# Three engines in hardware loops, DMA buffers moved to a 512-byte boundary, and a finer last load, in a decode kernel that streams a KV cache

## Chip, cores, metric

The kernel runs on one core of a Trainium2 chip. The metric is the device time of one execution in microseconds (us). A ratio is the mean time of one kernel's runs over the mean time of the other's runs in the same rounds, so it is not quite the ratio of the medians that are quoted beside it.

## The reference

One decode step, batch 2, one query position: an attention branch over a cache of 32768 keys and values (8 KV heads, 32 query heads), and a small MLP branch that gates its result.

```python
def _A_ref(x, k_cache, v_cache, wq, wo):        # caches: (2, 8, 32768, 128) bf16
    q = ((x @ wq).reshape(B, Sq, Hq, Dh)).transpose(0, 2, 1, 3)
    k = jnp.repeat(k_cache, rep, axis=1); v = jnp.repeat(v_cache, rep, axis=1)
    p = _softmax(jnp.einsum("bhqd,bhkd->bhqk", q, k) * (Dh ** -0.5))
    o = jnp.einsum("bhqk,bhkd->bhqd", p, v)
    return o.transpose(0, 2, 1, 3).reshape(B, Sq, Hq * Dh) @ wo
xn = _layernorm(A_x)
return A_x + _A_ref(xn, ...) * _silu(_B_ref(xn, ...))   # _B_ref: the MLP branch
```

K and V are 16 groups (batch x KV head) of 8.4 MB each. With the weights, 280.5 MB have to be read once.

## The kernel before

SyncE issues all large loads, in the order wq, w3, w4, K0, V0, K1, V1, ... K15, V15, wo. For one group, VectorE transposes K in 16 pieces, TensorE makes the scores, ScalarE the exponentials, VectorE transposes them, TensorE multiplies by V, and a short chain of copies, small matmuls and VectorE operations turns the sum into a column of `oX`. After the last group `oX` is multiplied by wo. TensorE runs 15 groups in a hardware loop and the last one unrolled; VectorE and ScalarE are unrolled over all 16.

```python
WO_PARTS = [(0, 4, 0, 2048), (4, 7, 0, 2048), (7, 8, 0, 2048)]
...
kbuf = pers.tile([128, 3 * SLOT], BF16, name="kbuf")     # first tile of the pool
vbuf = pers.tile([128, 2 * SLOT], BF16, name="vbuf")
...                                                       # SyncE
wait(sp, k_h2)
load_v(0)
for m in range(1, NG):
    wait(sp, (p_t, NT * (m - 1) + NR))                    # K's shared slot is free
    load_k(m)
    wait(sp, (p_o, m))                                    # V of the group before is used up
    load_v(m)
wait(sp, (p_t, NT * last))
for i, (g0, g1, c0, c1) in enumerate(WO_PARTS):
    d_wo[i].after(sp.dma_start(out=wo3[:, g0:g1, c0:c1], in_=wos[:, g0:g1, c0:c1]), 16)
...                                                       # VectorE, unrolled
for m in range(NG):
    for i in range(NPART):
        ...
        for r in range(NR):
            n = NT * m + NR * i + r
            wait(dve, (p_t, n + 1 - T_BUFS))
            dve.transpose(out=Ts[n % T_BUFS]..., in_=kt...).then_inc(s_t, 1)
    ...
...                                                       # TensorE
with pe.Fori(0, last):
    scores()
    values(lambda h: take(pe, s_v, 16) if h == 0 else None)
scores()
values(lambda h: wait(pe, (d_vl[h], 16)))
wait(pe, k_oX)
for i, (g0, g1, c0, c1) in enumerate(WO_PARTS):
    wait(pe, (d_wo[i], 16))
    ...                                                   # 16 matmuls a group of wo
```

`take(eng, sem, n)` waits until a semaphore is at least n and takes n off it, so that the same code can run for every group.

The softmax here doesn't subtract the row's maximum and nothing guards it: scores larger than these inputs give would overflow.

## Time and profile before

| | before |
|---|---|
| median of 4 runs | 661.09 us (660.90 to 661.62) |
| span of the profiled run | 659.8 us |
| load queue, share of 16 DMA engines' span | 98.5% |
| instruction packets inside the span (q8 + q14) | 5 + 6 |
| last V half used from | 645.00 us |
| `oX` complete | 652.44 us |

The page of the profile. First the busy time of each engine, then the row of 40 slices for the DMA engines (9 is 90% busy or more), then the DMA queues: q1 carries the loads, q8 and q14 carry instructions.

```profile
PE 393.7 (60%) x2684; PEld 165.5 (25%) x2684; DVE 337.0 (51%) x428; ACT 50.3 (8%) x152; POOL 5.7 (1%) x18
...
DMA  8999999999999999999999999999999999999994
...
q1 hardware_dynamic: 6408, 280.50, 98.5%
q8 instruction: 5, 0.08, 0.1%
q14 instruction: 6, 0.05, 0.0%
```

No compute engine is near its limit, the DMA engines are. Between 3 and 650 us their mean busy share is 1.00, as the windows show (DMA share and GB/s are the last two columns):

```profile
3.00:650.00 647.00, 388.65 (x2547) 160.90 (x2548) 334.69 (x418) 50.13 (x152) 3.95 (x8) 0.81 1.00 432
```

The end of the kernel, from the timeline (start in us, duration, engine, line, operation; in brackets the idle time before it and what ended it). L503 is the product with V, L473 completes `oX`, L540 is the product with wo:

```profile
645.00 3.59 PE L503 MATMUL bank<-vbuf,pt 128*16 128x512 bf16 x32 [5.08 <-DMA vbuf<-in_A_v_cache_dram]
...
652.27 0.17 DVE L473 TENSOR_REDUCE oX<-xm 128x4 bf16<-128x16 f32 x1
...
652.50 3.58 PE L540 MATMUL bank<-kbuf,oX 128*2 128x128 bf16 x128 [0.47 <-DVE oX L473]
```

TensorE waits 5 us for the last half of V, and everything after is a chain. The chain that ended last says the same, and that wo is not waited for:

```profile
652.27 0.18 DVE oX L473
652.45 0.04 issue
652.50 3.61 PE bank L540 x96
```

Two things are not on the page but in the trace's records of completion counts and of DMA packets. First the counts. The trace has 16 counts for each load of K, V and weights, as many as there are chains of load packets (below), and a load is used when the last of them has come: the last V half has its first count at 640.80 us and its 16th at 644.96, and TensorE starts on it at 645.00. I take one count for one DMA engine. So for each load there is a time when the 9th engine is done and one when the 16th is. Their difference, here called the lag, is how far the slowest engine is behind the middle:

```
kernel before, in us        load 1 (K0)   10th   11th   20th   21st   29th   30th   34th (last V half)
lag, 16th minus 9th count       1.5        1.5    1.9    1.9    2.9    2.9    3.9     4.0
VectorE instruction packets:  48 us            232 us        424 us        604 us
```

The loads are 19.35 us apart, and the lag grows only in the load in which a VectorE instruction packet arrives. (The queues are put down to engines by the doses below: unrolling VectorE takes q14 from 2 packets to 7, unrolling TensorE q8 from 4 to 22.)

Second, the packets. Their records name no engine, but from 22.5 to 640 us each packet begins within 0.05 us of the end of another, so the sixteen chains of packets, one for each DMA engine, can be followed. This is a stretch of the chain with the VectorE packet at 232 us (packets of 4 bytes left out):

```
start, us   took, ns   queue   bytes      one DMA engine of the kernel before
  230.093       2422   q1      65536
  232.512        333   q14      8192      instructions of VectorE
  232.833       3080   q1      65536      0.66 us longer than the others
  235.916       2419   q1      65536
```

The packet's own time and the lengthening of the load packet behind it together cost this engine 0.98 us. The VectorE packets at 48, 232, 424 and 604 us all lie in this one chain; the one at 188 us lies in another, and costs that engine 0.68 us.

### The profile page before, as it was taken

How to read it: one execution, taken by the hardware profiler on the slowest of the kernel's cores; microseconds unless marked ns; L12 is line 12 of the kernel's file. 1: busy time of each engine (PE TensorE's matmuls, PEld its weight loads, DVE VectorE, ACT ScalarE, POOL GpSimd, SP SyncE). 2: the span in 40 equal slices, each digit the busy share in tenths (PEclk: the TensorE clock that was granted, in tenths of full speed). 3: DMA queues.
4: the chain of work that ended last, by engine and by line, in shares of the span. 5: the costliest groups of instructions: out<-in, count | busy, mean ns of one | idle time of the engine just before them, and what ended most of it. 6: DMA issues, size and time to landing. Idle time of an engine off the chain costs nothing. (4 is left out here: it accounts for less than half of the span.)

```text
span 659.8 us, 6521 instructions
## 1 busy us (share of the span) xinstructions
PE 393.7 (60%) x2684; PEld 165.5 (25%) x2684; DVE 337.0 (51%) x428; ACT 50.3 (8%) x152; POOL 5.7 (1%) x18
## 2 busy tenths in 40 slices
PE   0538195683829558282865828376481947648765
PEld 0513132231313223031322303132131322213223
DVE  2347191744809165380926539083562908447650
ACT  0111001010100101010010101001010010101000
POOL 1200000000000000000000000000000000000000
PEclk9999787785978769597885959779596976959795
DMA  8999999999999999999999999999999999999994
GB/s 366 434 443 441 434 445 421 421 445 433 441 442 405 441 434 441 441 445 401 441 433 445 441 413 429 438 441 441 441 401 445 433 445 437 417 429 430 421 421 197
DMA packets 6443, 280.64 MB, mean 425 GB/s; under 512 B 664, under 2 KB 672, under 8 KB 1696
## 3 DMA queue, kind: packets, MB, share of 16 engines
q1 hardware_dynamic: 6408, 280.50, 98.5%
q8 instruction: 5, 0.08, 0.1%
q14 instruction: 6, 0.05, 0.0%
q10 hardware_dynamic: 24, 0.01, 0.0%
HBM read 280.50 MB, written 0.00 MB: 425 GB/s over the span
## 5 line engine op out<-in xcount | busy, mean ns | idle before, releaser
L486 PE MATMUL bank<-T,z 128*128 128x512 bf16 x1024 | 283.1, 428 | 184.7 <-PEq L45 179.6
L449 DVE STREAM_TRANSPOSE T<-kbuf 128x1024 int32<-128x1024 int32 x256 | 290.6, 1206 | 150.5 <-DMA kbuf<-in_A_k_cache_dram 150.5
L486 PEld LDWEIGHTS bank<-T,z 128*128 128x128 bf16 x1024 | 99.3, 104 | 362.0 <-issue 283.6
L503 PE MATMUL bank<-vbuf,pt 128*16 128x512 bf16 x1024 | 68.2, 426 | 5.1 <-DMA vbuf<-in_A_v_cache_dram 5.1
L466 DVE RECIPROCAL rec<-bank 128x4 f32<-128x4 f32 x16 | 2.9, 182 | 114.2 <-PE bank L513 114.2
L423 ACT ACTIVATE ep<-bank 128x512 bf16<-128x512 f32 x32 | 19.1, 598 | 482.2 <-PE bank L486 482.2
L503 PEld LDWEIGHTS bank<-vbuf,pt 128*16 128x16 bf16 x1024 | 26.4, 98 | 38.8 <-issue 12.6
L457 DVE STREAM_TRANSPOSE pt<-ep 128x512 bf16<-128x512 bf16 x32 | 22.1, 691 | 20.2 <-ACT ep L423 20.2
L496 PE MATMUL bank<-sm,ones_f 128*128 128x4 f32 x64 | 9.4, 252 | 27.6 <-PEq L45 27.6
L513 PE MATMUL bank<-sel_o,ob 128*128 128x4 f32 x128 | 17.2, 258 | 12.5 <-PEq L45 12.5
L513 PEld LDWEIGHTS bank<-sel_o,ob 128*128 128x128 f32 x128 | 16.3, 199 | 20.5 <-issue 20.5
L496 PEld LDWEIGHTS bank<-sm,ones_f 128*128 128x128 f32 x64 | 8.5, 192 | 35.4 <-issue 35.4
L431 ACT COPY ob<-bank 128x512 f32<-128x512 f32 x16 | 9.4, 586 | 87.6 <-PE bank L503 87.6
L411 ACT COPY z<-qr 32x16 bf16<-32x16 bf16 x64 | 12.6, 197 | 0.6
L286 PE MATMUL bank<-ident,xn_bf 2*128 2x2 bf16 x4 | 0.3, 166 | 16.7 <-POOL x L277 16.7
L519 PE MATMUL bank<-on,sel_r 128*128 128x4 bf16 x64 | 3.9, 164 | 9.0 <-PEq L45 9.0
L423 ACT ACTIVATION_READ_ACCUMULATOR ep<-bank 128x1 f32 x32 | 6.3, 198 | 0.2
L470 DVE TENSOR_TENSOR xm<-bank,mask 128x16 f32<-128x16 f32 x16 | 2.8, 175 | 6.8 <-PE bank L519 6.8
L245 DVE CAST xf<-x_bf 128x512 f32<-128x512 bf16 x1 | 0.4, 427 | 11.4 <-DMA x_bf<-in_A_x_dram 11.4
L462 DVE TENSOR_SCALAR sm<-sel_h,rs 128x4 f32<-128x4 f32 x32 | 6.0, 188 | 0.0
L519 PEld LDWEIGHTS bank<-on,sel_r 128*128 128x128 bf16 x64 | 2.9, 97 | 9.9 <-issue 9.9
L322 PE MATMUL bank<-xT,kbuf 128*128 128x2 bf16 x128 | 3.6, 165 | 2.0 <-DVE xT L316 2.0
(64 smaller groups left out, 50.2 us busy)
## 6 DMA issues: line engine op xcount, KB each, us to landing
kbuf<-in_A_k_cache_dram SPq DMA_DIRECT2D x2, 4096.0 KB, 23.7
vbuf<-in_A_v_cache_dram SPq DMA_DIRECT2D x2, 4096.0 KB, 28.9
kbuf<-in_A_wq_dram SPq DMA_DIRECT2D x1, 4096.0 KB, 12.2
vbuf<-in_B_w_dram SPq DMA_DIRECT2D x2, 1792.0 KB, 17.9
kbuf<-in_A_wo_dram SPq DMA_DIRECT2D x1, 2048.0 KB, 38.3
kbuf<-in_A_wo_dram SPq DMA_DIRECT2D x1, 1536.0 KB, 41.5
kbuf<-in_A_wo_dram SPq DMA_DIRECT2D x1, 512.0 KB, 42.1
kbuf<-in_A_k_cache_dram SPq DMA_DIRECT2D x15, 27.7
```

The lines of the kernel that those rows point to most:

```text
L322: i = pe.matmul(qT_ps[:, h * B:(h + 1) * B], lhsT=wq3[:, k, h * Dh:(h + 1) * Dh], rhs=xT[:, k, :], start=(k == 0), stop=(k == DK - 1),)
L411: i = act.copy(out=z[32 * j:32 * j + 32, :, :, c:c + rep], in_=qr[32 * j:32 * j + 32, :, :, b, g * rep:(g + 1) * rep],)
L423: act.activation(out=eps_[i][:, :], in_=sc[i][:, :], func=ACT.Exp, scale=inv_sqrt_dh, accum_out=rss[NPART * (m % 2) + i][:, :],)
L431: act.copy(out=ob[:, :], in_=o[:, :]).then_inc(s_ob, 1)
L449: dve.transpose(out=Ts[n % T_BUFS][:, :].rearrange("p (b t k) -> p t b k", b=NB, t=RT), in_=kt[:, r * W:(r + 1) * W].rearrange("p (t b k) ...
L457: dve.transpose(out=pts[h][:, :, :].rearrange("p r (t h) -> p t r h", h=rep), in_=eps_[i][:, :].rearrange("p (t r h) -> p t r h", r=NR, h= ...
L462: dve.tensor_scalar_mul(out=sms[h][:, :], in0=sel_h[:, :], scalar1=rss[NPART * (m % 2) + i][:, 0:1]).then_inc(s_p, 1)
L486: last_mm = pe.matmul(sc[i][:, :], lhsT=z[:, nb, e, zc:zc + 128], rhs=Tb[:, nb, :, e], start=(r == 0 and nb == 0 and e == 0), stop=(r == N ...
L496: pe.matmul(S, lhsT=ones_f[:, :], rhs=sms[h][:, :], start=(h == 0), stop=(h == NPART - 1))
L503: last_mm = pe.matmul(o[32 * j:32 * j + VT * rep, :], lhsT=pts[h][:, r, a * VT * rep:(a + 1) * VT * rep], rhs=vt[:, u * VT:(u + 1) * VT, : ...
L513: last_mm = pe.matmul(oT, lhsT=ob[:, t * Dh:(t + 1) * Dh], rhs=sel_o[:, t, :], start=(t == 0), stop=(t == VT - 1))
L519: last_mm = pe.matmul(xp[:, r, :], lhsT=sel_r[:, r, :, :].rearrange("p j w -> p (j w)"), rhs=on[:, :], start=True, stop=True,)
```

## The change

Its intent: run TensorE, VectorE and ScalarE over all 16 groups in hardware loops (VectorE two groups a turn, because K's halves alternate), so that their code is not streamed during the run; put the DMA buffers on a 512-byte boundary; cut wo's last pieces finer, so that less work follows the last landing. All waits inside the loops become semaphores that are taken down, and since each matmul of this program signals one semaphore, one-column matmuls (`mark`) signal the others.

```diff
-WO_PARTS = [(0, 4, 0, 2048), (4, 7, 0, 2048), (7, 8, 0, 2048)]
+WO_PARTS = [(0, 2, 0, 2048), (2, 4, 0, 2048), (4, 5, 0, 2048), (5, 6, 0, 2048), (6, 7, 0, 2048),
+            (7, 8, 0, 1024), (7, 8, 1024, 1536), (7, 8, 1536, 2048)]
+    pers.tile([128, PAD // 4], F32, name="pad")          # PAD = 384
     kbuf = pers.tile([128, 3 * SLOT], BF16, name="kbuf")
 ...
-            wait(sp, (p_t, NT * (m - 1) + NR))
+            sp.wait_ge(p_k, m)
             load_k(m)
-            wait(sp, (p_o, m))
+            sp.wait_ge(p_o, m)
             load_v(m)
 ...
-        emit_z(0)
-        for m in range(NG):
+        with act.Fori(0, NG) as m:
+            for j in range(4):  ...  in_=qr[..., bass.ds(m * rep, rep)]
 ...
-        for m in range(NG):
-            ...  wait(dve, (p_t, n + 1 - T_BUFS))
+        with dve.Fori(0, NG // 2) as t:
+            for odd in range(2):
+                group(odd, t)          # inside: take(dve, s_tf), take(dve, s_k[i], 16), ...
 ...
-        with pe.Fori(0, last):
-            scores(); values(...)
-        scores(); values(...)
+        with pe.Fori(0, NG):
+            ...  mm.then_inc(s_tf if r < NR - 1 else s_sc, 1)
+            ...  mark(s_tf); if i == 0: mark(p_k)
```

In the built programs kbuf starts at byte 16512 of a partition before (128 past a multiple of 512) and at 16896 (a multiple) after.

More of the change, by code (lines that the diff above doesn't have):

```diff
@@ L18 @@
 T_BUFS = 4
+PAD = 384
 GELU_C = 0.7978845608028654
 EPS = 1e-5
-WO_PARTS = [(0, 4, 0, 2048), (4, 7, 0, 2048), (7, 8, 0, 2048)]
+WO_PARTS = [(0, 2, 0, 2048), (2, 4, 0, 2048), (4, 5, 0, 2048), (5, 6, 0, 2048), (6, 7, 0, 2048), (7, 8, 0, 1024), (7, 8, 1024, 1536), (7, 8, 1536, 2048)]
 class Count:
@@ L100 @@
     pts = [pers.tile([128, NR, RT * rep], BF16, name=f"pt{i}") for i in range(NPART)]
-    rss = [pers.tile([128, 1], F32, name=f"rs{i}") for i in range(2 * NPART)]
+    rss = [pers.tile([128, 1], F32, name=f"rs{i}") for i in range(NPART)]
     sms = [pers.tile([128, rep], F32, name=f"sm{i}") for i in range(NPART)]
@@ L107 @@
     xm = pers.tile([128, NQ, rep], F32, name="xm")
-    oX = pers.tile([128, Hkv, NQ, B], BF16, name="oX")
+    oX = pers.tile([128, B * Hkv * NQ], BF16, name="oX")
     ident = pers.tile([128, 128], BF16, name="ident")
@@ L125 @@
     q_sb = pers.tile([128, B, Hq], BF16, name="q_sb")
-    qr = pers.tile([128, NB, 2, B, Hq], BF16, name="qr")
+    qr = pers.tile([128, NB, 2, B * Hq], BF16, name="qr")
     hf = pers.tile([128, FK * B], F32, name="hf")
@@ L149 @@
     qr_ps = sc[1][:, 0:NB * 2 * B * Hq].rearrange("p (n e c) -> p n e c", n=NB, e=2)
+    mark_ps = treg_b[0:1, 0:1]
     hT = xp_b[:, 0:FK * B]
@@ L158 @@
         d_x, d_wq, d_w3, d_w4 = (Count(nc, n) for n in ("d_x", "d_wq", "d_w3", "d_w4"))
-        d_k = [Count(nc, f"d_k{i}") for i in range(2)]
-        d_kl = [Count(nc, f"d_kl{i}") for i in range(NPART)]
-        s_v = nc.alloc_semaphore("s_v")
-        d_vl = [Count(nc, f"d_vl{i}") for i in range(NPART)]
+        s_k = [nc.alloc_semaphore(f"s_k{i}") for i in range(NPART)]
+        s_v = [nc.alloc_semaphore(f"s_v{i}") for i in range(NPART)]
         d_wo = [Count(nc, f"d_wo{i}") for i in range(len(WO_PARTS))]
@@ L165 @@
         v_, p_, a_, g_ = (Count(nc, n) for n in ("v_", "p_", "a_", "g_"))
-        s_t, s_z, s_p, s_ob, s_on = (nc.alloc_semaphore(n) for n in ("s_t", "s_z", "s_p", "s_ob", "s_on"))
-        p_t, p_o, p_x, a_e, v_p = (Count(nc, n) for n in ("p_t", "p_o", "p_x", "a_e", "v_p"))
+        s_t, s_tf, s_z, s_sc, s_e, s_p, s_o, s_ob, s_x, s_on, s_d, s_r, p_k, p_o = (
+            nc.alloc_semaphore(n)
+            for n in ("s_t", "s_tf", "s_z", "s_sc", "s_e", "s_p", "s_o", "s_ob", "s_x", "s_on", "s_d", "s_r", "p_k",
+                      "p_o")
+        )
         def V(inst):
@@ L193, with load @@
         )
+        def load(cache, dst, sems, m):
+            src = row_view(cache, *groups[m])
+            if m < last:
+                sp.dma_start(out=dst, in_=src).then_inc(sems[0], 16)
+                sp.sem_inc(sems[1], 16)
+            else:
+                for c in range(NPART):
+                    w = slice(c * SLOT, (c + 1) * SLOT)
+                    sp.dma_start(out=dst[:, w], in_=src[:, w]).then_inc(sems[c], 16)
         def load_k(m):
             base = (m % 2) * SLOT
-            src = row_view(A_k_cache, *groups[m])
-            if m < last:
-                d_k[m % 2].after(sp.dma_start(out=kbuf[:, base:base + 2 * SLOT], in_=src), 16)
-            else:
-                for c in range(NPART):
-                    d_kl[c].after(
-                        sp.dma_start(
-                            out=kbuf[:, base + c * SLOT:base + (c + 1) * SLOT],
-                            in_=src[:, c * SLOT:(c + 1) * SLOT],
-                        ), 16,
-                    )
-        def load_v(m):
-            src = row_view(A_v_cache, *groups[m])
-            if m < last:
-                sp.dma_start(out=vbuf[:, :], in_=src).then_inc(s_v, 16)
-            else:
-                for c in range(NPART):
-                    d_vl[c].after(
-                        sp.dma_start(out=vbuf[:, c * SLOT:(c + 1) * SLOT], in_=src[:, c * SLOT:(c + 1) * SLOT]), 16
-                    )
+            load(A_k_cache, kbuf[:, base:base + 2 * SLOT], s_k, m)
+        def load_v(m):
+            load(A_v_cache, vbuf[:, :], s_v, m)
         load_k(0)
@@ L341 @@
             dve.tensor_copy(
-                out=qr[:, :, :, :, :].rearrange("p n e b h -> p (n e b h)"),
+                out=qr[:, :, :, :].rearrange("p n e c -> p (n e c)"),
                 in_=qr_ps.rearrange("p n e c -> p (n e c)"),
@@ L390 @@
         k_g4 = V(dve.tensor_mul(out=g4[0:QP, :], in0=t_f[0:QP, :], in1=sig[0:QP, :]))
-        NT = NPART * NR
         wait(sp, k_h2)
@@ L396 @@
         for m in range(1, NG):
-            wait(sp, (p_t, NT * (m - 1) + NR))
+            sp.wait_ge(p_k, m)
             load_k(m)
-            wait(sp, (p_o, m))
+            sp.wait_ge(p_o, m)
             load_v(m)
-        wait(sp, (p_t, NT * last))
         wos = A_wo.rearrange("(g p r) d -> p g (r d)", p=128, r=NQ)
@@ L404 @@
             d_wo[i].after(sp.dma_start(out=wo3[:, g0:g1, c0:c1], in_=wos[:, g0:g1, c0:c1]), 16)
-        def emit_z(m):
-            b, g = groups[m]
+        wait(act, k_z0, k_qr)
+        with act.Fori(0, NG) as m:
             for j in range(4):
@@ L412, in emit_z, with then, group @@
                     out=z[32 * j:32 * j + 32, :, :, c:c + rep],
-                    in_=qr[32 * j:32 * j + 32, :, :, b, g * rep:(g + 1) * rep],
+                    in_=qr[32 * j:32 * j + 32, :, :, bass.ds(m * rep, rep)],
                 )
             i.then_inc(s_z, 1)
-        wait(act, k_z0, k_qr)
-        emit_z(0)
-        for m in range(NG):
             for i in range(NPART):
-                wait(act, (p_t, NT * m + NR * (i + 1)), (v_p, NPART * (m - 1) + i + 1))
-                a_e.after(
-                    act.activation(
-                        out=eps_[i][:, :], in_=sc[i][:, :], func=ACT.Exp, scale=inv_sqrt_dh,
-                        accum_out=rss[NPART * (m % 2) + i][:, :],
-                    )
-                )
-            if m < last:
-                emit_z(m + 1)
-            wait(act, (p_o, m + 1))
+                take(act, s_sc)
+                act.activation(
+                    out=eps_[i][:, :], in_=sc[i][:, :], func=ACT.Exp, scale=inv_sqrt_dh, accum_out=rss[i][:, :]
+                ).then_inc(s_e, 1)
+            take(act, s_o)
             act.copy(out=ob[:, :], in_=o[:, :]).then_inc(s_ob, 1)
         W = RT * NB * 32
-        wait(dve, k_sh, k_mask)
-        for m in range(NG):
-            b, g = groups[m]
-            hs = halves(m)
+        def then(inst):
+            inst.then_inc(s_d, 1)
+            take(dve, s_d)
+        def group(odd, t):
+            hs = halves(odd)
             for i in range(NPART):
-                u = m % 2 + hs[i]
+                u = odd + hs[i]
                 kt = kbuf[:, u * SLOT:(u + 1) * SLOT].bitcast(I32)
-                if m == last:
-                    wait(dve, (d_kl[hs[i]], 16))
-                elif i == 0:
-                    wait(dve, (d_k[m % 2], 16 * (m // 2 + 1)))
+                take(dve, s_k[i], 16)
                 for r in range(NR):
-                    n = NT * m + NR * i + r
-                    wait(dve, (p_t, n + 1 - T_BUFS))
+                    take(dve, s_tf)
                     dve.transpose(
-                        out=Ts[n % T_BUFS][:, :].rearrange("p (b t k) -> p t b k", b=NB, t=RT),
+                        out=Ts[(NR * i + r) % T_BUFS][:, :].rearrange("p (b t k) -> p t b k", b=NB, t=RT),
                         in_=kt[:, r * W:(r + 1) * W].rearrange("p (t b k) -> p t b k", b=NB, t=RT),
@@ L454, with mark @@
                 h = hs[i]
-                wait(dve, (a_e, NPART * m + i + 1), (p_o, m))
-                v_p.after(
-                    dve.transpose(
-                        out=pts[h][:, :, :].rearrange("p r (t h) -> p t r h", h=rep),
-                        in_=eps_[i][:, :].rearrange("p (t r h) -> p t r h", r=NR, h=rep),
-                    )
-                )
-                dve.tensor_scalar_mul(
-                    out=sms[h][:, :], in0=sel_h[:, :], scalar1=rss[NPART * (m % 2) + i][:, 0:1]
-                ).then_inc(s_p, 1)
-            wait(dve, (p_x, 2 * m + 1))
-            k = V(dve.reciprocal(out=rec[:, :], in_=S))
-            wait(dve, k)
+                take(dve, s_e)
+                dve.transpose(
+                    out=pts[h][:, :, :].rearrange("p r (t h) -> p t r h", h=rep),
+                    in_=eps_[i][:, :].rearrange("p (t r h) -> p t r h", r=NR, h=rep),
+                )
+                dve.tensor_scalar_mul(out=sms[h][:, :], in0=sel_h[:, :], scalar1=rss[i][:, 0:1]).then_inc(s_p, 1)
+            take(dve, s_x)
+            then(dve.reciprocal(out=rec[:, :], in_=S))
             dve.tensor_mul(out=on[:, :], in0=oT, in1=rec[:, :]).then_inc(s_on, 1)
-            wait(dve, (p_x, 2 * m + 2))
-            k = V(dve.tensor_mul(out=xm[:, :, :], in0=xp, in1=mask[:, :, :]))
-            wait(dve, k)
+            take(dve, s_x)
+            then(dve.tensor_mul(out=xm[:, :, :], in0=xp, in1=mask[:, :, :]))
             with nc.allow_low_precision(reason="three of the four terms are zero, the fourth is bf16"):
-                k_oX = V(dve.tensor_reduce(out=oX[:, g, :, b], in_=xm[:, :, :], axis=AX.X, op=ALU.add))
-        def scores():
+                dve.tensor_reduce(
+                    out=oX[:, bass.ds(t * (2 * NQ) + odd * NQ, NQ)], in_=xm[:, :, :], axis=AX.X, op=ALU.add
+                ).then_inc(s_r, 1)
+        wait(dve, k_sh, k_mask)
+        dve.sem_inc(s_tf, T_BUFS)
+        with dve.Fori(0, NG // 2) as t:
+            for odd in range(2):
+                group(odd, t)
+        def mark(sem):
+            pe.matmul(mark_ps, lhsT=ident[:, 0:1], rhs=ident[:, 0:1], start=True, stop=True).then_inc(sem, 1)
+        wait(pe, (g_, g_.n), k_mask)
+        with pe.Fori(0, NG):
             take(pe, s_z)
@@ L485, in scores @@
                         for e in range(2):
-                            last_mm = pe.matmul(
+                            mm = pe.matmul(
                                 sc[i][:, :], lhsT=z[:, nb, e, zc:zc + 128], rhs=Tb[:, nb, :, e],
@@ L490, in scores @@
                             )
-                    last_mm.then_inc(p_t.sem, 1)
-        def values(v_ready):
+                    mm.then_inc(s_tf if r < NR - 1 else s_sc, 1)
+                mark(s_tf)
+                if i == 0:
+                    mark(p_k)
             take(pe, s_p, NPART)
@@ L497, in values @@
             for h in range(NPART):
-                v_ready(h)
+                take(pe, s_v[h], 16)
                 vt = vbuf[:, h * SLOT:(h + 1) * SLOT].rearrange("p (t d) -> p t d", d=Dh)
@@ L502, in values @@
                     j = u % 4
-                    last_mm = pe.matmul(
+                    mm = pe.matmul(
                         o[32 * j:32 * j + VT * rep, :],
@@ L509, in values @@
                     )
-            last_mm.then_inc(p_o.sem, 1)
+            mm.then_inc(s_o, 1)
+            mark(p_o)
             take(pe, s_ob)
             for t in range(VT):
-                last_mm = pe.matmul(
+                mm = pe.matmul(
                     oT, lhsT=ob[:, t * Dh:(t + 1) * Dh], rhs=sel_o[:, t, :], start=(t == 0), stop=(t == VT - 1)
                 )
-            last_mm.then_inc(p_x.sem, 1)
+            mm.then_inc(s_x, 1)
             take(pe, s_on)
             for r in range(NQ):
-                last_mm = pe.matmul(
+                mm = pe.matmul(
                     xp[:, r, :], lhsT=sel_r[:, r, :, :].rearrange("p j w -> p (j w)"), rhs=on[:, :],
@@ L522, in values @@
                 )
-            last_mm.then_inc(p_x.sem, 1)
-        wait(pe, (g_, g_.n), k_mask)
-        with pe.Fori(0, last):
-            scores()
-            values(lambda h: take(pe, s_v, 16) if h == 0 else None)
-        scores()
-        values(lambda h: wait(pe, (d_vl[h], 16)))
-        wait(pe, k_oX)
+            mm.then_inc(s_x, 1)
+        oXv = oX[:, :].rearrange("p (b g r) -> p g r b", b=B, g=Hkv)
+        pe.wait_ge(s_r, NG)
         for i, (g0, g1, c0, c1) in enumerate(WO_PARTS):
@@ L540 @@
                         mm = pe.matmul(
-                            s_ps[32 * n:32 * n + B, :], lhsT=oX[:, g, r, :], rhs=wo3[:, g, c:c + QW],
+                            s_ps[32 * n:32 * n + B, :], lhsT=oXv[:, g, r, :], rhs=wo3[:, g, c:c + QW],
                             start=(g == 0 and r == 0), stop=(g == Hkv - 1 and r == NQ - 1),
```

## The prediction

> **What bounds the kernel now.** The DMA engines. Queue table: load queue 98.5% of 16 engines' span (280.5 MB, 425 GB/s over the span); slices: DMA at 9 from the second to the last but one. Packet records: their time over 16 engines is 650 of 659.8 us; from 3 to 650 us all are busy. A 64 KB packet takes 2421 ns (27.07 GB/s per engine, 433 GB/s for 16). In the waits, VectorE waits 150 us for K; the queue's own waits are for buffers, but every K or V load is issued 8 to 13 us before the queue runs out.
>
> The rest: 2 us at the start, and the tail. The packet records show the last V half finished by most engines at 640.3 us, by four at 641.2 to 642.0, and by one only at 644.4. For wo: most by 652.1, one at 654.5. The records of the two instruction queues (page: 5 packets on q8, 6 on q14) lie where single load packets become 0.4 to 0.66 us longer (8 places up to 605 us, about 4.6 us in all). A load counts as landed when its slowest engine is done, so V's last half is seen at 645.0 us (timeline). Then a fixed chain: values 3.6 us, copy, transposes and scale to oX at 652.45, wo matmuls 3.6 us, output: 659.8.
>
> [...] The trace agrees that blocks are fetched (16 and 8 KB packets), but here they are taken from the bounding resource.
>
> **What the change does.**
> - Loops on VectorE and ScalarE remove most of their streamed code: the fetches at 188, 232, 424 and 605 us go, each worth 0.4 to 0.66 us on one engine (2.3 us). Those up to 70 us stay. The slowest engine should end V at about 642 instead of 644.4: -2.4 us at most, on the critical path.
> - Alignment: [...] I expect 0 to 5 ns a packet, 0 to 1.3 us.
> - Finer wo parts: the chain shows the 96 last wo matmuls running without a wait after oX. Worth about 0.
> - Added: four one-column matmuls a group (estimate 0.1 to 0.2 us each), semaphore takes on VectorE and ScalarE, and the z copies (0.8 us) moved behind the ob copy. All falls into about 8 us of slack per group (VectorE is idle 8 to 11 us before each K), so 0. In the last group a few takes lie on the tail: +0.3 us.
>
> **Sum.** 661.2 - 2.4 - 0.6 + 0.3 = 658.5 us. Range 656.3 to 661.0. Faster by over 2%: 0.01; same: 0.98; slower: 0.01.
>
> **What would show it.** Fewer instruction packets on q14; 64 KB packets at 2415 to 2421 ns; the load queue still above 98%; the last V half landing at about 642.5; the chain still values, copy, oX, wo; oX-to-end unchanged.
>
> **What would make it wrong.** A loop body that doesn't stay in instruction memory and is fetched every turn (more packets, slower). [...] A fetch stall at TensorE's loop exit. The straggling engine having another cause than fetches.

The alignment term: its 0 to 5 ns a packet (0 to 1.3 us over the 280.5 MB, which are worth 268 packets of 64 KB an engine) and the 0.6 us taken from that are the author's guess. So is the 0.3 us on the tail. The 0.1 to 0.2 us for a one-column matmul was given without its source; in the profile before, a matmul with 4 columns takes 164 ns (L519), and those of the change came out at 164 ns too (L464 of the kernel after).

## The result

| | before | after |
|---|---|---|
| median of 4 runs | 661.09 us (660.90 to 661.62) | 657.61 us (657.20 to 658.71) |
| ratio, 95% interval | | 0.9949 (0.9932 to 0.9966) |
| span of the profiled run | 659.8 us | 655.9 us |
| load queue, share | 98.5% | 99.0% |
| mean time of a 64 KB load packet | 2422.6 ns | 2419.8 ns |
| lag at the last V half | 4.0 us | 1.5 us |

The change saves half a per cent, 3.5 us by the medians. The page after, the same rows:

```profile
PE 391.5 (60%) x2716; PEld 168.8 (26%) x2748; DVE 337.2 (51%) x428; ACT 71.3 (11%) x167; POOL 5.6 (1%) x18
...
DMA  8999999999999999999999999999999999999996
...
q1 hardware_dynamic: 6744, 280.50, 99.0%
q8 instruction: 4, 0.07, 0.0%
q14 instruction: 2, 0.02, 0.0%
```

The instruction packets on q14 fell from 6 to 2. ScalarE became 21 us busier, which the prediction did not have: in its loop a table load precedes the first copy of every turn.

```profile
L406 ACT ACT_TABLE_LOAD x16 | 20.5, 1283 | 0.3
```

It costs nothing, since ScalarE is 11% busy and the last of these loads is done at 613.0 us, 3 us before the scores of the last group begin. The end, from the timeline of the kernel after (L495 is the product with V, L452 completes `oX`, L527 is the product with wo):

```profile
641.77 1.90 PE L495 MATMUL bank<-vbuf,pt 128*16 128x512 bf16 x32 [1.89 <-PEq L46]
...
647.15 0.17 DVE L452 TENSOR_REDUCE oX<-xm 128x16 f32 x1 [0.24 <-DVEq L46]
...
647.38 2.73 PE L527 MATMUL bank<-kbuf,oX 128*2 128x128 bf16 x96 [0.79 <-DVE oX L452]
650.39 0.40 PE L527 MATMUL bank<-kbuf,oX 128*2 128x128 bf16 x16 [0.29 <-DMA kbuf<-in_A_wo_dram]
```

The last V half is used 3.2 us earlier than before (641.77 against 645.00). `oX` then comes 5.6 us later instead of 7.4, chiefly because the same matmuls ran at another granted clock. The windows (granted clock is the third last column) over the product with V, first of the kernel before, then of the kernel after:

```profile
645.00:649.00 4.00, 3.59 (x32) 0.98 (x32) 0.00 (x0) 0.35 (x1) 0.00 (x0) 0.50 1.03 410
```

```profile
641.70:643.70 2.00, 1.90 (x33) 0.86 (x33) 0.00 (x0) 0.00 (x0) 0.00 (x0) 1.00 1.03 424
```

But this didn't shorten the whole: now TensorE waits for wo, and the chain that ended last runs through the last wo part:

```profile
639.11 12.57 DMA kbuf<-in_A_wo_dram
651.68 0.04 issue
651.73 0.26 PE bank L527 x4
```

Is that the rule for the kernel after? No. In a second profile of it (run after_again below) the clock was 0.50 over the product with V (3.6 us again), the wo matmuls followed `oX` in one go, and the span was the same (656.0 us):

```profile
641.40:645.00 3.60, 3.58 (x33) 1.14 (x33) 0.00 (x0) 0.00 (x0) 0.00 (x0) 0.50 1.03 419
```

```profile
648.68 3.36 PE L527 MATMUL bank<-kbuf,oX 128*2 128x128 bf16 x128 [0.79 <-DVE oX L452]
```

The two paths to the end, over V and over wo, are within about a microsecond of each other, and in these two profiles the path over V is the longer where the clock was low.

### The profile page after: what moved, and what is told of

It reads as the page before. It is cut to its first block, busy times and chain, and to the rows that moved or that the text cites. A ratio compares the mean times of both kernels' runs of the same rounds, so it can differ in the third digit from the quotient of the medians. Undisturbed runs are those within 1.5% of the kernel's fastest.

```text
span 655.9 us, 7180 instructions
## 1 busy us (share of the span) xinstructions
PE 391.5 (60%) x2716; PEld 168.8 (26%) x2748; DVE 337.2 (51%) x428; ACT 71.3 (11%) x167; POOL 5.6 (1%) x18
## 5 line engine op out<-in xcount | busy, mean ns | idle before, releaser
L477 PE MATMUL bank<-T,z 128*128 128x512 bf16 x992 | 274.2, 425 | 178.5 <-PEq L46 174.5
L495 PE MATMUL bank<-vbuf,pt 128*16 128x512 bf16 x1024 | 73.2, 449 | 1.9 <-PEq L46 1.9
L495 PEld LDWEIGHTS bank<-vbuf,pt 128*16 128x16 bf16 x1024 | 27.8, 102 | 39.5 <-issue 21.7
L406 ACT COPY z<-qr 32x16 bf16 x64 | 12.9, 201 | 0.7
L512 PE MATMUL bank<-on,sel_r 128*128 128x4 bf16 x64 | 3.9, 165 | 12.6 <-PEq L46 12.6
L464 PE MATMUL bank<-ident 128*1 128x1 bf16 x64 | 8.3, 164 | 0.0
L464 PEld LDWEIGHTS bank<-ident 128*1 128x1 bf16 x64 | 4.0, 81 | 16.0 <-issue 14.2
```

The lines of the kernel that those rows point to most:

```text
L406: i = act.copy(out=z[32 * j:32 * j + 32, :, :, c:c + rep], in_=qr[32 * j:32 * j + 32, :, :, bass.ds(m * rep, rep)],)
L464: pe.matmul(mark_ps, lhsT=ident[:, 0:1], rhs=ident[:, 0:1], start=True, stop=True).then_inc(sem, 1)
L477: mm = pe.matmul(sc[i][:, :], lhsT=z[:, nb, e, zc:zc + 128], rhs=Tb[:, nb, :, e], start=(r == 0 and nb == 0 and e == 0), stop=(r == NR - 1 ...
L495: mm = pe.matmul(o[32 * j:32 * j + VT * rep, :], lhsT=pts[h][:, r, a * VT * rep:(a + 1) * VT * rep], rhs=vt[:, u * VT:(u + 1) * VT, :].rea ...
L512: mm = pe.matmul(xp[:, r, :], lhsT=sel_r[:, r, :, :].rearrange("p j w -> p (j w)"), rhs=on[:, :], start=True, stop=True,)
```

## The experiments

The theory: this kernel's end follows the slowest of its 16 DMA engines. Streamed VectorE code is fetched through one of these engines, always the same (four packets of four in the kernel before), and each fetch puts it further behind; loops stop that. Rivals: the gain is that of alignment; of the finer wo; or of something else in the loops (the takes, the marks, TensorE's last group no longer unrolled).

All 12 runs gave the right result. Times of one job share the runs of the kernel before. The three jobs had before at 661.15, 661.51 and 661.16 us (the second ran on another chip). Between jobs the ratios are compared; where their intervals overlap, a difference is likely at most.

| run | change from | median us | ratio to before |
|---|---|---|---|
| before_pad | before | 659.58 | 0.9977 (0.9963 to 0.9990) |
| before_wo | before | 661.38 | 0.9996 (0.9983 to 1.0010) |
| loops_only | after | 659.46 | 0.9977 (0.9964 to 0.9991) |
| after_oldwo | after | 658.09 | 0.9958 (0.9944 to 0.9971) |
| after_nopad | after | 658.86 | 0.9971 (0.9958 to 0.9985) |
| after_again | after | 657.47 | 0.9946 (0.9932 to 0.9959) |
| dve_unrolled | after | 661.45 | 0.9999 (0.9985 to 1.0012) |
| pe_unrolled | after | 661.47 | 0.9998 (0.9984 to 1.0012) |
| off224 | after | 660.34 | 0.9984 (0.9970 to 0.9997) |
| off256 | after | 657.51 | 0.9946 (0.9932 to 0.9959) |
| tiles_off | after | 657.67 | 0.9952 (0.9938 to 0.9965) |
| compact_q | after | 670.07 | 1.0134 (1.0119 to 1.0150) |

For each, three numbers from the completion counts of its profiled run: the mean of the 29 distances between the first 30 K and V loads for the middle (9th) engine, the lag at the last V half, and when this half was complete. The last column is the rest of the span.

```
                9th, us apart   lag at last V   last V landed   from there to the end
before             19.353            4.0            644.96            14.8
before_pad         19.326            3.0            643.07            14.8
before_wo          19.353            4.2            645.32            14.2
loops_only         19.353            1.7            642.78            15.1
after_nopad        19.353            1.7            642.60            14.5
after_oldwo        19.324            1.4            641.27            14.9
after              19.332            1.5            641.64            14.3
after_again        19.320            1.5            641.26            14.7
off256             19.324            1.5            641.34            14.7
tiles_off          19.323            1.3            641.17            14.6
off224             19.360            2.1            643.38            15.1
dve_unrolled       19.323            4.3            644.91            14.3
pe_unrolled        19.416            1.7            644.34            15.0
```

The rest of the span is 14.2 to 15.1 us in all of them. The kernels differ above all in when the last V half lands. The row of pe_unrolled misleads: there the 9th engine is itself one of eight late ones (see below).

### One part at a time: loops_only, before_pad, after_nopad, after_oldwo, before_wo

loops_only is the kernel after with

```diff
-    pers.tile([128, PAD // 4], F32, name="pad")
-WO_PARTS = [... 8 parts ...]
+WO_PARTS = [(0, 4, 0, 2048), (4, 7, 0, 2048), (7, 8, 0, 2048)]
```

> Loops alone, without pad and with the old wo parts. Fetch theory: keeps 2.3 to 3 us of the 3.5 us (658.1 to 658.8), the last V half landing at 642 to 642.6, q14 with 2 packets. If loops are not the cause: 660.5 to 661.5.

Measured: 659.46 us, 1.7 us below before; the size is somewhat below what was expected (2.3 to 3). The last V half landed at 642.78, 2.2 us before the old time, and the lag is 1.7 instead of 4.0 with the middle engine's pace unchanged (19.353). So the loops act on the slowest engine alone. Part of it is lost behind that: the way from V's landing to the end is 15.1 instead of 14.8 us in these profiles.

before_pad is the kernel before with

```diff
+    pers.tile([128, 384 // 4], F32, name="pad")
     kbuf = pers.tile([128, 3 * SLOT], BF16, name="kbuf")
```

> The kernel before with the pad alone. Fetch theory: 0.5 to 1.0 us faster than before (660.1 to 660.6), packets at 2418 ns, the straggling engine still about 4 us behind the others at the last V half, q14 with about 6 packets. Alignment theory: 2.5 us or more faster, and the straggler gone.

Measured: 659.58 us, 1.6 us below before, more than the 0.5 to 1.0 that was expected, and the straggler is not gone. The mean 64 KB packet fell from 2422.6 to 2419.5 ns; the middle engine's loads are 19.326 instead of 19.353 us apart, 0.9 us in 32 loads. The other part is in the lag, 3.0 instead of 4.0: with the buffers aligned the slow engine catches up by 0.1 to 0.2 us between two fetches, four times in the run, which it doesn't do without (lag at loads 1, 10, 11, 20, 21, 29: 1.5, 1.3, 1.6, 1.3, 2.3, 2.1). Why it can is not settled by these runs.

after_nopad is the kernel after with

```diff
-    pers.tile([128, PAD // 4], F32, name="pad")
```

> The kernel after with the 384-byte pad taken out, so that kbuf starts 128 bytes off a multiple of 512 again. Fetch theory: the gain of 3.5 us is nearly all in the loops, so this is 0.5 to 1.0 us slower than the kernel after (658.1 to 658.6), with 64 KB packets back at 2421 ns from 2418 (3 ns x 272 packets per engine = 0.8 us) and two fetches on q14. Alignment theory: most of the gain goes, 660 or more.

Measured: 658.86 us, 1.25 us above the kernel after (by ratio: 0.9971 against 0.9949; the two are of different jobs, and their intervals just overlap). The loads are back at 19.353. The loss is a little above the expected range; it is not "most of the gain".

after_oldwo is the kernel after with

```diff
-WO_PARTS = [... 8 parts ...]
+WO_PARTS = [(0, 4, 0, 2048), (4, 7, 0, 2048), (7, 8, 0, 2048)]
```

> The kernel after with the three old wo parts. In the kernel after, TensorE waits for wo's last parts. Fetch theory: the last part is 16 matmuls instead of 4 after the landing (0.45 instead of 0.26 us) and there are fewer small packets (about 0.1 us per engine), so 0 to 0.4 us slower than the kernel after. Rival (finer wo gives the gain): 2 us or more slower, near 660.

Measured: 658.09 us, 0.5 us above the kernel after. The pair of the same job, after_nopad against loops_only, differs in the same edit and gives 0.6 us. The intervals of the ratios overlap in both pairs, so this half microsecond is likely, not shown. (The 0.1 us for small packets in the expectation fits the packet records of the kernel after: 1 KB takes 46 ns, 2 KB 84 and 4 KB 159.) The profile has a place for it: TensorE did 64 of the 128 wo matmuls only after the second part had landed (1.17 us of waiting), with 1.88 us of matmuls behind that.

```profile
647.00 1.88 PE L527 MATMUL bank<-kbuf,oX 128*2 128x128 bf16 x64 [0.79 <-DVE oX L452]
650.05 1.88 PE L527 MATMUL bank<-kbuf,oX 128*2 128x128 bf16 x64 [1.17 <-DMA kbuf<-in_A_wo_dram]
```

before_wo is the kernel before with the eight parts of the change.

> The kernel before with the eight wo parts alone. There oX comes at 652.45 us, wo lands at 654 and TensorE runs all 128 wo matmuls in one go after oX, so finer parts have nothing to shorten: 661.1, within 0.3 us. If finer parts help by themselves (0.5 us as between the kernel after and its variant with three parts): 660.5 or less.

Measured: 661.38 us beside 661.51, no difference, as expected, but the reason given is not what its profile shows. TensorE did not run all 128 wo matmuls in one go: it waited for the late parts of wo, and the chain that ended last runs through wo's last part.

```profile
654.18 1.59 PE L540 MATMUL bank<-kbuf,oX 128*2 128x128 bf16 x32 [0.33 <-DMA kbuf<-in_A_wo_dram]
```

The straggling engine, which no cut of wo removes, delivers the last part at 655.46 us here and at 654.98 us in the kernel before. Why finer parts seem to help the kernel after and not this one is not shown further.

Together: loops 1.7, pad 1.6, and both 3.1 us (after_oldwo against before in the same job: 658.09 and 661.15). The two parts add up, 3.3 against 3.1.

### Doses of streamed code: dve_unrolled, pe_unrolled

```diff
-        with dve.Fori(0, NG // 2) as t:
+        for t in range(NG // 2):
```

> The kernel after with VectorE's loop unrolled again (same instructions, same waits, same order; only the code is streamed). Fetch theory: the 8 KB fetches on q14 come back (five or so instead of two), one engine ends the last V half about 3 us behind the others, and of the loops' 1.7 us most is lost: 658.6 to 659.6, against 657.6 for the kernel after. If the loops gained by something else (the takes, the one-column marks, TensorE's unpeeled last group): no change from 657.6.

Measured: 661.45 us, 3.5 us slower than the kernel after by the ratios (0.9999 against 0.9946). All of the change's gain is gone, though the pad and the finer wo are still there, and every instruction, wait and mark of the loops too. The loss is above the expected 1 to 2 us. There are 7 instead of 2 packets on q14:

```profile
q8 instruction: 4, 0.07, 0.0%
q14 instruction: 7, 0.06, 0.0%
```

The one-off fetches at about 55 and 645 us are in the kernel after too; the five new ones come at 155, 255, 364, 466 and 566 us. With the 15th count beside the 16th it can be seen whom they hit:

```
dve_unrolled, us     load 6   load 11  load 12  load 17  load 18  load 22  load 23  load 27  load 28
16th minus 9th         1.5      1.6      2.6      2.4      3.4      3.3      4.2      4.1      5.1
15th minus 9th         1.4      1.4      1.5      1.5      1.4      1.4      1.4      1.4      1.4
new packet, at us      155 (in load 7)   255               364               466               566
```

One engine falls behind by about 1 us with every packet (the first of the five brings it only level with the slowest of the others, which are 1.4 us late anyway), and the other fifteen stay where they were. By the packet records all five lie in one engine's chain; each costs it 0.31 us of its own and about 0.55 us of lengthening (the count steps up by 1.0 and comes down by about 0.1 before the next packet). (From load 31 on the middle engine comes 0.6 us later itself, which is why the lag at the last V half reads 4.3.) The kernel before has the same picture: its 15th count is 1.4 to 1.5 us late in every load, its 16th climbs to 4.0. The packet at 188 us, ScalarE's to judge by its place outside VectorE's rhythm and in another engine's chain, moves neither.

The second dose is

```diff
-        with pe.Fori(0, NG):
+        for _ in range(NG):
```

> A dose: the kernel after with TensorE's loop unrolled, about 290 instructions a group, so some 16 to 20 fetches of 16 KB more. Fetch theory: each costs one DMA engine 0.5 to 1.6 us (16 KB are 0.6 us of its time), so if they all fall on one engine 8 to 25 us slower, and if they rotate over 16 engines about 1 us slower than the kernel after; the number of 16 KB packets on q8 rises from 4 to about 20 in any case. If fetches are hidden: 657.6.

Measured: 661.47 us, 3.4 us slower than the kernel after by the ratios, between the two cases. There are 18 more packets of 16 KB on q8, inside the expected 16 to 20, which were the author's estimate:

```profile
q8 instruction: 22, 0.36, 0.2%
q14 instruction: 2, 0.02, 0.0%
```

The lag at the last V half is 1.7, hardly more than in the kernel after, and the middle engine's loads are 19.416 instead of 19.324 to 19.332 us apart. That looks as if all engines had become slower, but they had not. All sixteen counts of the last V half, in us after the first of them:

```
after        0.0 0.1 0.1 0.1 0.1 0.1 0.1 0.2 0.2 0.2 0.2 0.3 0.7 1.3 1.6 1.7
pe_unrolled  0.0 0.1 0.1 0.2 0.2 0.3 0.4 0.8 2.9 3.0 3.0 4.0 4.3 4.4 4.5 4.6
```

The first count comes at 639.93 us in the kernel after and at 639.76 here: eight engines have lost nothing, and the other eight are 2.9 to 4.6 us late. The 9th is the first of these, so the lag hides them. The chains of packets say the same. TensorE's 21 fetches up to there go round eight engines in a fixed order, so that three engines have had two of them and five have had three, as the counts show. A fetch takes 0.88 to 0.97 us, and the load packet behind it is about 0.5 us longer: 1.4 us of one engine's time. TensorE's three early fetches likewise make the three engines that are 1.3 to 1.7 us late in the kernel after (their chains were followed in before, loops_only and after_again). So this dose acts as VectorE's does, through the slowest engine: the last V half lands at 644.34 instead of 641.64 us. The 18 packets more cost about what VectorE's five do because they are shared out.

### What alignment needs: off256, off224, tiles_off, and the partner after_again

after_again is the kernel after, unchanged.

> The kernel after, unchanged, as the partner of the other three on the same chip: 657.3 to 658.0, ratio 0.994 to 0.996.

Measured: 657.47 us, as expected. off256:

```diff
-PAD = 384
+PAD = 128
```

> The kernel after with a pad of 128 bytes: kbuf and vbuf start on a multiple of 256 that is not one of 512. If 256 is what counts [...]: as the kernel after, 64 KB packets at 2418 ns, loads landing 19.30 us apart, within 0.3 us of the partner. If 512 counts: as without the pad, 19.35 us apart, about 1.2 us slower.

Measured: 657.51 us and 19.324 us between loads: as its partner. A start on a multiple of 256 bytes was enough here; one on a multiple of 512 (the partner: 657.47 us, 19.320 us between loads) gave nothing more. off224:

```diff
-PAD = 384
+PAD = 96
```

> The kernel after with a pad of 96 bytes, so that kbuf, vbuf and the rest start 224 bytes past a multiple of 256 instead of 0 (kernel before: 128). [...] If only aligned or not matters: 2421 to 2422 ns and 658.9.

Measured: 660.34 us, by ratio 0.9 us slower than the pad taken out (another job; the intervals overlap). The time is above the 658.9 us of the branch, the packets hardly above its 2421 to 2422 ns: their mean is 2423.1 ns against 2422.1 without the pad, 1 ns. The loads are 19.360 instead of 19.353 us apart, 0.2 us in 32 loads. The rest of the difference is a lag of 2.1 instead of 1.7 us (from load 1 on, so not a matter of pace) and a way to the end of 15.1 instead of 14.5 us in this profile. So the packets take longer at 224 bytes past a multiple of 256, as they do at 128 (2423.1 and 2422.1 ns against 2419.8 in the kernel after), and whether 224 costs more than 128 is not shown. tiles_off:

```diff
     vbuf = pers.tile([128, 2 * SLOT], BF16, name="vbuf")
+    pers.tile([128, 32], F32, name="pad2")
```

> The kernel after with 128 bytes more after vbuf: the DMA targets kbuf and vbuf stay aligned, every tile that the engines alone use is 128 bytes off, as in the kernel before. If alignment acts on the DMA writes alone: within 0.3 us of the partner. If it acts on what the engines read and write: 1 us or more slower.

Measured: 657.67 us and 19.323 us between loads. The partner has 657.47 and 19.320. So what the pad gains here it gains at kbuf and vbuf, which the DMA writes; the tiles of the engines lay 128 bytes off without a loss that shows.

### An attempt at a faster kernel, which failed: compact_q

Three fetches of TensorE's code before the groups (at 29, 36 and 69 us) remain. The attempt makes the 128 unrolled q matmuls a loop:

```diff
-        for h in range(Hq):
-            for k in range(DK):
-                i = pe.matmul(qT_ps[:, h * B:(h + 1) * B], lhsT=wq3[:, k, h * Dh:(h + 1) * Dh], ...)
-        k_q = P(i)
+        with pe.Fori(0, Hq // 4) as h4:
+            for j in range(4):
+                for k in range(DK):
+                    i = pe.matmul(qT_ps[:, bass.ds(h4 * (4 * B) + j * B, B)],
+                                  lhsT=wq3[:, k, bass.ds(h4 * (4 * Dh) + j * Dh, Dh)], ...)
+        k_q = P(pe.matmul(mark_ps, lhsT=ident[:, 0:1], rhs=ident[:, 0:1], ...))
```

> The kernel after with TensorE's 128 unrolled q matmuls as a loop of 8 turns of 16, 112 matmuls less code: one 16 KB fetch less before the groups (q8 from 4 packets to 3). A load lands when its slowest engine is done, and each of the three early fetches delays another engine by 1.1 to 1.6 us: if the maximum counts, taking one away changes little, within 0.4 us of the partner. If each fetch costs the whole by itself: 0.5 us or more faster. If a loop's start-up delays the first V load: slower.

Measured: 670.07 us, 12.6 us slower than its partner. One packet on q8 less, as intended, and the lag still 1.4 us: taking one of three fetches away does not move the maximum. But here each of the 128 matmuls, whose addresses now come from registers, comes with a register instruction of its own (46 ns in the median). The matmuls follow each other at 124 ns (median) instead of 27, and 0.6 us passes between two turns: 2.64 us a turn of 16, 165 ns a matmul on average.

```profile
L320 PEldq FUSED_REGOPS  x128: 42/46/79, 21.7 to 42.2; - x128
L320 PEld LDWEIGHTS bank<-xT,kbuf x128: 102/105/105, 21.8 to 42.3; 128*128 x128
```

The 128 matmuls take from 21.8 to 42.5 us, where the unrolled ones in the kernel after take 3.6 us in all. V0's load waits for what follows them, is issued at 50.16 instead of 32.40 us, and the DMA queue runs dry. The window from 41 to 51 us, first of compact_q, then of the kernel after:

```profile
41.00:51.00 10.00, 6.97 (x129) 6.19 (x128) 2.13 (x10) 1.92 (x4) 0.00 (x0) 1.00 0.01 2
```

```profile
41.00:51.00 10.00, 6.47 (x18) 2.49 (x20) 7.88 (x7) 0.00 (x0) 0.00 (x0) 1.00 0.97 419
```

Ten microseconds at 2 GB/s and nothing later gives them back, because everything later runs at the DMA engines' pace (9 in every later slice but the last). The loops of the change don't have this cost where it would matter: their matmuls and transposes have constant addresses, and only ScalarE's four z copies and VectorE's `oX` take a register in each group (46 ns in the median for each of ScalarE's 48 register instructions, L406 of the kernel after).

## Why the prediction was right

The time was 657.6 us, inside 656.3 to 661.0 and 0.9 us under the point of 658.5. The bound was named rightly: the load queue had 98.5% before and has 99.0% after, and the loads run back to back in both. The terms of the sum were less good than the sum. That it came so near is in part luck: measured alone, the loops gained 0.7 us less and the alignment 1.0 us more than predicted, and the finer wo perhaps 0.5 us that was not predicted.

- **Loops, predicted -2.4 us at V, "at most".** Measured alone (loops_only): V lands 2.2 us earlier, the time falls by 1.7 us. The loops were not fetched again with every turn: q14 has 2 packets and q8 has 4 in the whole span after. The mechanism is shown by the counts and by the dose: one engine, about 1 us per VectorE packet. Two sizes inside it were wrong and compensated each other. I took 0.4 to 0.66 us per fetch from the lengthening of single packets; it is 1.0 us, since the fetch's own 0.33 us come on top. And I counted four fetches on the straggler, with ScalarE's; ScalarE's at 188 us fell on another engine, and VectorE's first ones are hidden behind the 1.5 us by which the next slowest engine is late.
- **Alignment, predicted 0 to 1.3 us, -0.6 in the sum.** Measured alone: 1.6 us; on top of the loops 1.4 (after_oldwo against loops_only, in one job). This term was mis-sized. 0.9 us of it is the pace, as predicted in kind (2.8 ns a packet, and 0.03 us a load). The rest in before_pad is that the straggler catches up, which I didn't foresee.
- **Finer wo parts, predicted about 0.** Measured 0.5 and 0.6 us in two pairs whose intervals overlap, so likely but not shown; and 0 on the kernel before. The step that failed is "the chain still values, copy, oX, wo" and "oX-to-end unchanged": in the kernel after the way from `oX` to the end is 8.6 instead of 7.3 us, and its chain goes through wo's landing. I had read "no wait for wo" off the kernel before, without asking how far wo was from being one: its second and third part landed at 653.75 and 654.98 us, and their first matmuls ran at 654.16 and 655.44, only 0.4 to 0.5 us later.
- **Takes, marks, z copies: 0 in the groups, +0.3 on the tail.** Right: with these in place the loads of loops_only are as close together as before (19.353 us in both), and its way from V's landing to the end is 15.1 instead of 14.8 us.
- **The tail as "a fixed chain".** Wrong: at a granted clock of 0.50 the 32 matmuls after V take 3.6 us, at 1.00 they take 1.9. It did not change the span between the two profiles of the kernel after (655.9 and 656.0 us), since wo's landing then takes over.

What the fetching engine itself loses was not measured here. What its fetches take from the DMA engines is not hidden: dve_unrolled loses 3.5 us by streaming one engine's code. And the writes of the loads show a cost of a start 128 bytes off (2422.6 against 2419.8 ns for a 64 KB packet), while a multiple of 256 bytes sufficed (off256: 657.51 us beside 657.47).

What stays open: why the load packet behind a fetch becomes 0.5 to 0.7 us longer, so that a fetch costs an engine about 1.0 us (VectorE) or 1.4 us (TensorE) when its bytes are worth 0.3 and 0.6 (an estimate at a load packet's rate, 64 KB in 2.42 us); why VectorE's fetches keep to one engine and TensorE's go round eight; why an aligned straggler catches up; and whether the finer wo parts gain half a microsecond.

## What to carry to other kernels

When the DMA engines are the bound (98.5% here), ask for the slowest of the sixteen, not for the mean (here it ended the last V half 4.0 us after the middle one): look at how the last completion counts of a load spread, and whether the spread grows. Look at all sixteen: a distance from the middle one is blind when eight are late (pe_unrolled: it reads 1.7 us where eight are 2.9 to 4.6 us late). Streamed instructions were DMA traffic here, small in bytes and dear in time (about 1.0 us of one engine for 8 KB of VectorE's), so in such a kernel a loop with constant addresses can beat unrolling (by 3.5 us in dve_unrolled); with addresses from registers, weigh what they cost (compact_q: 2.64 instead of 0.45 us for 16 small matmuls) against what the loop saves. A path that is "not waited for" before a change may be the bound after it: compute its distance.
